# Transposing the tokens of six of eight experts on VectorE, from gathered quarter rows

## The chip, the cores and the metric

The kernel runs on one core of one Trainium2 chip. The core has TensorE (PE in the profile, with its weight loads as PEld), VectorE (DVE), ScalarE (ACT), GpSimd (POOL) and SyncE (SP), which run side by side and wait for each other by semaphores. The metric is the device time of one execution in microseconds (us).

## The reference

Attention over pooled keys and values makes 4608 rows x of 512 columns. A gate gives each row 8 logits; the pairs of row and expert are taken in falling order of their logits until each of the 8 experts has its 576 rows. Each expert then applies its two matrices to its rows.

```python
cap = N // E                      # 4608 // 8 = 576
for idx in np.argsort(-logits.flatten()):
    tok, e = (int(idx) // E, int(idx) % E)
    if assigned[tok] >= 0 or counts[e] >= cap:
        continue
    assigned[tok] = e
    counts[e] += 1
for e in range(E):
    mask = assigned == e
    h = np.maximum(x[mask] @ w1[e], 0.0)      # (576, 512) @ (512, 1024)
    out[mask] = h @ w2[e]                     # (576, 1024) @ (1024, 512)
```

## The kernel before

**Three parts.** The attention (class `Attention`) writes x to DRAM as `xd`. The routing (class `Routing`) finds one full expert after another, by a search that counts rows above thresholds: VectorE compares, TensorE counts, VectorE decides, several rounds per expert. It ends with the expert's number `eid` and with `rows`, the 576 row numbers as a tile of 128 partitions and 5 columns, tile t in column t (the fifth tile has 64 rows). The number of an expert below is its place in this order. The experts (class `Experts`) then multiply.

**One expert.** `gather` (L1031) fetches the 576 rows of `xd` into `xg` by five indirect DMAs that GpSimd issues, one token per partition, 2 KB each. TensorE contracts over partitions, so x has to be turned: `xt` (L1060) transposes tile t by four TensorE transposes of 128x128 into the PSUM tile `tp` (two buffers), chunk j of the result holding columns 128j to 128j+127. Every fp32 operand is split in two parts of TensorE's faster format: ScalarE copies `tp` to `xh` and VectorE writes the rest, `tp - xh`, to `xl`. The weights are split likewise, w1 into `w1h` and `w1l` and w2 into `w2h` and `w2l`, in eight pieces of 512 columns each (class `Pieces` in `experts`). `load_1` loads w1 so that partition p of chunk j holds row 128j + p, as x's columns lie.

`stage1` (L1075) computes the 1024 hidden columns in blocks f of 128, first for tokens 0 to 255, then for 256 to 575: 12 matmuls for each block (three products of high and low parts, four chunks j), into one of five PSUM banks `h`. After each block ScalarE writes `hh` and VectorE `hl`. `stage2` (L1113) multiplies tile by tile with w2, 24 matmuls each for four tiles, and a last half tile; ScalarE copies the result to `yt` (two buffers) and GpSimd scatters it by row number.

**The order.** Nothing reorders the program: each engine runs its instructions in the order in which the program issues them. The generators `stage1` and `stage2` yield after each matmul with an estimate of its time, and `experts` keeps a planned clock `now` and a planned end of VectorE's work `dve`. Between matmuls `advance` (L1263) puts in the next step of the routing of the following expert when its inputs are planned to be ready, `turns` (L1333) puts in the next tile's transpose, `Pieces.by` a piece of the weights, and `flush` those VectorE instructions that `later` has put off. `turns` asks that the rows are planned to have arrived (6.5 + 1.3t after the row numbers are known), that 1.4 us have passed since the last tile, and that a routing step has just been put in (`fresh`), that routing is over (`through`), or that the tile's limit `late` is reached. So tiles 0 to 2 of the next expert fall into the second stage of the present one, tiles 3 and 4 into its own first stage. The row numbers are taken into use only when the present expert's five tiles are turned, as there is one `xg`. No routing step starts while an `xl` is still put off (`first`, L1314).

The row numbers come out in `Routing.close` (L715): nine matmuls (L779) give sums in which every number stands at one place, `cp` holds them for the 18 groups of 32 places in two parts v, and eight matmuls with shifted copies of the matrix `spread` (L798) put four groups above each other in the partitions, which gives `rows`.

Of the kernel before, what the change touches and what calls it, by code (L numbers as in the profile page):

```python
# [9 lines left out]
F32 = mybir.dt.float32  # L10
# [413 lines left out]
class Routing:  # L424
# [56 lines left out]
    def more(self):  # L481
# [10 lines left out]
        nc.vector.tensor_scalar(self.spread[:, 96:128], t, 0.0, None, op0=OP.is_equal)  # L492

        self.blk = cst.tile([128, 20, NC], BF, name="blk")
        nc.scalar.activation(self.blk[:, :18], self.i36[:, 1:19, None].to_broadcast([128, 18, NC]), AF.Copy)
# [219 lines left out]
    def close(self, k, last):  # L715
# [58 lines left out]
        for b0, b1 in halves:  # L774
# [19 lines left out]
            t0, t1 = b0 // 4, b1 // 4  # L794
            ps = self.psum()
            for g in range(4):
                for v in range(2):
                    nc.tensor.matmul(ps[:, :t1 - t0], self.spread[:, 96 - 32 * g:224 - 32 * g], cpv[:, v, :, g],  # L798
                                     start=(g == v == 0), stop=(g == 3 and v == 1))
# [184 lines left out]
class Experts:  # L984
# [27 lines left out]

    def load_1(self, eid, q0=0, q1=4):
        nc = self.nc
        r = nc.sync.value_load(eid[0:1, 0:1], min_val=0, max_val=7)
        if q0 == 0:
            self.raw1.append(self.buf("raw1", [128, 4, 1024]))
        src = self.w1[ds(r, 1)].rearrange("o (j p) f -> p (o j) f", p=128)
        for q in range(q0, q1):
            nc.sync.dma_start(self.raw1[-1][:, *self.part(q)], src[:, *self.part(q)])  # L1020

    def load_2(self, eid):
# [4 lines left out]
        for i in range(0, 8, 2):  # L1027
            nc.sync.dma_start(raw[:, i:i + 2], src[:, i:i + 2])
        self.raw2.append(raw)

    def gather(self, rows, t0, t1):  # L1031
# [27 lines left out]

    def xt(self, t, name="tp", bufs=2, later=lambda after, t, f: f()):  # L1060

# [5 lines left out]
        ps = self.psA.tile([128, 4, 128], F32, name=name, bufs=bufs)  # L1067
        for j in range(4):
            nc.tensor.transpose(ps[:, j, :n], self.xg[:n, t, 128 * j:128 * j + 128], self.ident[:n, :n])  # L1069
        o = slice(128 * t, 128 * t + n)  # L1070
        nc.scalar.activation(self.xh[:, :, o], ps[:, :, :n], AF.Copy)  # L1071
        xl, xh = self.xl[:, :, o], self.xh[:, :, o].bitcast(F32)
        later(1.3, 0.65, lambda: nc.vector.tensor_tensor(xl, ps[:, :, :n], xh, op=OP.subtract))  # L1073

# [127 lines left out]
def experts(ctx, tc, g, R, xd, w1, w2, out, ident, cap, keep):  # L1202
# [15 lines left out]
    now, dve, ready = 0.0, 0.0, 0.0  # L1218

    def later(after, t, f):  # L1220

        waiting.append((now + after, t, f))
# [8 lines left out]
    def step(e):  # L1231

        nonlocal now, ready, dve, fresh, coming, through
        if held:
# [6 lines left out]
        if what == "id":  # L1241

            if p > e or p and pieces[p - 1].l < 8:
                held.append((p, crit, t, what))
                return False
            X.load_1(R.eid, 0, 4 if p else 2)
            eids[p] = R.eid
        elif what == "rows":
            if p and turned[p - 1] < 5:
                held.append((p, crit, t, what))  # L1250
                return False
            X.gather(R.rows, *R.found)
            if R.found[1] == 5:
# [9 lines left out]
    def advance(e, t, quiet=False):  # L1263

        nonlocal now, fresh
        now += t
        fresh = False
        while True:
            if waiting and waiting[0][0] <= now:
                flush(len(waiting) - 1)  # L1270
            elif ready > now or quiet or first(e) or not step(e):
                break
# [47 lines left out]
    def turn(e, t, name="tp", bufs=2):  # L1320

        nonlocal now
        now = max(now, since[e, "rows"] + 6.0 + 1.3 * t) + 0.45
        flush(1)
        X.xt(t, name, bufs, later_low)
        turned[e] = t + 1
# [6 lines left out]
    def turns(e, upto, late):  # L1333

        nonlocal last
        t = turned.get(e, 5)
        if t < upto and due(e, "rows", 6.5 + 1.3 * t) and now >= last + 1.4 and (fresh or through or t < late):
            last = now
            turn(e, t)
# [15 lines left out]
    for i in range(4):  # L1355
        w1.next(i < 3)
    since[0, "rows"] = -7.0

    step(0)
# [9 lines left out]
    for e in range(8):  # L1369
# [5 lines left out]
        for n, dt in enumerate(X.stage1(later, not e)):  # L1375
# [5 lines left out]
            if n == (84 if e else 40):  # L1381
                for t in range(turned[e], 5):
                    turn(e, t)
            if n >= 64 and n % 2:
                w2.by((n - 70) // 14 if n > 70 else 0)
# [117 lines left out]
```

## Time and profile before

| | |
|---|---|
| Median of 3 runs | 611.87 us (611.85 to 612.09) |
| The profiled execution | 612.35 us, its span 609.9 us |
| Mean granted clock of TensorE | 0.984 |
| HBM traffic | 72.53 MB read, 18.87 MB written |
| Attention and the first routing | about the first 157 us |
| One expert, window of the trace | 57.7 us early, 54.4 us late |

The profile names a group of instructions by line, engine, operation and tiles. Its chain of work is followed back from the last instruction to what released each step. A matmul's duration is its passage through a pipelined array, so the distance between starts shows what it takes from the next. In the timeline an instruction's row has its start, its duration, and in brackets how long its engine had been idle and what ended that.

### The profile page before, as it was taken

To read this page: it belongs to the slowest core of one execution; us is meant where nothing else is said; L and a number is where in the kernel's file an instruction comes from. 1 tells how busy PE (TensorE), PEld (TensorE's weight loads), DVE (VectorE), ACT (ScalarE), POOL (GpSimd) and SP (SyncE) were. 2 spreads that over 40 slices of the span, in tenths; PEclk is the share of its full clock that TensorE was granted. 3 is DMA by queue.
4 is the path that set the end of the run, shared out by engine and by line. 5 is a ranking of instruction groups with operands and counts; after the bars stand their busy time and mean duration, and the time that the engine had idled before them with its cause. 6 is when DMAs were issued, how large, how long until landed. Compare 5 with 4: busy or idle time off the path is not lost.

```text
span 609.9 us, 11520 instructions
## 1 busy us (share of the span) xinstructions
PE 591.5 (97%) x4340; PEld 518.3 (85%) x4340; DVE 396.1 (65%) x1164; ACT 240.0 (39%) x562; POOL 177.3 (29%) x222
## 2 busy tenths in 40 slices
PE   8999999985999999999999999999999999999996
PEld 5999999983797799779977987898799889888975
DVE  7578888987885778767964976487367328503500
ACT  7444444461461434233432452255135325513411
POOL 2999999001200500420312301130221123011012
PEclk9999999995999999999999999999999999999999
DMA  8999972223531740616403701540081037014011
GB/s 353 419 420 423 397 274 82 77 100 98 167 116 31 254 147 22 213 62 219 134 35 116 284 1 52 207 174 18 36 323 57 34 120 278 2 52 166 1 40 43
DMA packets 32641, 92.23 MB, mean 151 GB/s; under 512 B 3488, under 2 KB 3488, under 8 KB 29888
## 3 DMA queue, kind: packets, MB, share of 16 engines
q1 hardware_dynamic: 21296, 62.92, 27.5%
q0 software_dynamic: 5952, 19.01, 9.2%
q10 hardware_dynamic: 5328, 9.48, 4.1%
q8 instruction: 35, 0.57, 0.4%
q14 instruction: 30, 0.25, 0.1%
HBM read 72.53 MB, written 18.87 MB: 150 GB/s over the span
## 4 chain that ended last, share of the span: by engine, by line
PE 81%; issue 7%; DVE 4%; DMA 3%; POOL 3%; ACT 1%; SPq 0%; POOLq 0%; ACTq 0%; another core or an unknown queue 0%; DVEq 0%
PE h L1093 32%; PE h L1127 25%; PE psa L272 6%; PE pss L227 5%; PE h L1132 4%; PE tp L1069 3%; DMA rawk<-in_k_dram 2%; PE pse L256 2%; PE rt L256 1%; PE rt L668 1%; DMA out_dram<-yt,rows 1%; PE rt L630 1%; DMA xg<-xd,rows 1%; PE rt L217 1%; DVE e L238 1%
## 5 line engine op out<-in xcount | busy, mean ns | idle before, releaser
L1127 PE MATMUL h<-w2l,hh 128*128 128x512 f32 x256 | 101.8, 398 | 0.0
L1127 PE MATMUL h<-w2h,hh 128*128 128x512 f32 x256 | 101.4, 396 | 0.3 <-PEq L1193 0.3
L1127 PE MATMUL h<-w2h,hl 128*128 128x512 f32 x256 | 101.5, 396 | 0.0
L1107 POOL DMA_INDIRECT out_dram<-yt,rows x29 | 30.3, 1045 | 232.3 <-ACT yt L1141 231.9
L1098 ACT ACTIVATE hh<-h 128x320 fp32r<-128x320 f32 (+1 forms) x128 | 52.5, 410 | 106.6 <-PE h L1093 103.3
L1093 PE MATMUL h<-xh,w1h 128*128 128x320 f32 (+1 forms) x512 | 93.2, 301 | 0.2 <-ACT xh L1071 0.2
L1093 PE MATMUL h<-xl,w1h 128*128 128x320 f32 (+1 forms) x512 | 93.4, 300 | 0.0
L1101 DVE SCALAR_TENSOR_TENSOR hl<-h,hh 128x320 fp32r<-128x320 f32 (+1 forms) x128 | 57.2, 451 | 53.1 <-ACT hh L1098 34.6
L1093 PE MATMUL h<-xh,w1l 128*128 128x320 f32 (+1 forms) x512 | 91.0, 298 | 0.0
L1093 PEld LDWEIGHTS h<-xh,w1h 128*128 128x128 f32 x512 | 75.7, 190 | 3.4 <-issue 2.7
L1093 PEld LDWEIGHTS h<-xl,w1h 128*128 128x128 f32 x512 | 76.1, 190 | 0.4
L1093 PEld LDWEIGHTS h<-xh,w1l 128*128 128x128 f32 x512 | 75.8, 189 | 0.0
L1037 POOL DMA_INDIRECT xg<-xd,rows x40 | 39.3, 982 | 101.9 <-DVE halves L806 52.7
L1141 ACT ACTIVATE yt<-h 128x512 f32<-128x512 f32 x32 | 19.1, 598 | 112.1 <-PE h L1127 67.4
L272 PE MATMUL psa<-vblk,eT 128*128 128x146 f32 (+3 forms) x390 | 59.9, 302 | 0.2
L1127 PEld LDWEIGHTS h<-w2h,hh 128*128 128x128 f32 x256 | 48.2, 188 | 9.3 <-issue 0.7
L1127 PEld LDWEIGHTS h<-w2l,hh 128*128 128x128 f32 x256 | 48.3, 189 | 8.8
L1127 PEld LDWEIGHTS h<-w2h,hl 128*128 128x128 f32 x256 | 48.2, 188 | 8.8
L272 PEld LDWEIGHTS psa<-vblk,eT 128*128 128x128 f32 (+1 forms) x390 | 50.9, 180 | 1.8 <-issue 0.3
L1049 DVE TENSOR_TENSOR w1l<-raw,w1h 128x512 fp32r<-128x512 f32 x64 | 41.7, 685 | 13.4 <-ACT w1h L1045 13.1
L1073 DVE TENSOR_TENSOR xl<-tp,xh 128x512 fp32r<-128x512 f32 (+1 forms) x40 | 25.3, 633 | 37.4 <-ACT xh L1071 37.3
L1058 DVE TENSOR_TENSOR w2l<-raw,w2h 128x512 fp32r<-128x512 f32 x64 | 43.2, 682 | 2.0 <-ACT w2h L1055 1.8
(224 smaller groups left out, 903.3 us busy)
## 6 DMA issues: line engine op xcount, KB each, us to landing
raw<-in_moe_w_dram SPq DMA_DIRECT2D x64, 512.0 KB, 6.3
xd<-xt ACTq DMA_DIRECT2D x36, 256.0 KB, 5.6
rawv<-in_v_dram SPq DMA_DIRECT2D x7, 1280.0 KB, 14.1
rawk<-in_k_dram SPq DMA_DIRECT2D x7, 1152.0 KB, 11.7
rawq<-in_q_dram SPq DMA_DIRECT2D x7, 1152.0 KB, 11.8
rawk<-in_k_dram SPq DMA_DIRECT2D x2, 576.0 KB, 4.7
rawv<-in_v_dram SPq DMA_DIRECT2D x1, 768.0 KB, 8.0
rawq<-in_q_dram SPq DMA_DIRECT2D x1, 640.0 KB, 9.0
```

The source lines that it names most:

```text
L227: nc.tensor.matmul(ps[cols, j // 2, 144 * (j % 2):144 * (j % 2) + 144], self.q_of(b, j, n, cols.stop - cols.start), self.kblk[b % 4][:, j] ...
L272: self.nc.tensor.matmul(o[h], self.eT[i][:, c, h], self.vblk[b % 4][:, self.BLOCKS[c]:self.BLOCKS[c + 1]], start=(c == cs[0]), stop=(c == ...
L1037: nc.gpsimd.indirect_dma_start(out=self.xg[:n, t, :], out_offset=None, in_=self.xd, in_offset=bass.IndirectOffsetOnAxis(ap=rows[:n, t:t + ...
L1049: self.nc.vector.tensor_tensor(l, raw, h.bitcast(F32), op=OP.subtract)
L1058: self.nc.vector.tensor_tensor(self.w2l[:, i], self.raw2[e][:, i], self.w2h[:, i].bitcast(F32), op=OP.subtract)
L1073: later(1.3, 0.65, lambda: nc.vector.tensor_tensor(xl, ps[:, :, :n], xh, op=OP.subtract))
L1093: nc.tensor.matmul(ps[:, :m], a[:, j, fs], b[:, j, o], start=(n == 0), stop=(n == 11))
L1098: nc.scalar.activation(hh[:, f, o], ps[:, :m], AF.Relu)
L1101: later(0.65, 0.4, lambda f=f, o=o, m=m, ps=ps: nc.vector.scalar_tensor_tensor(hl[:, f, o], ps[:, :m], 0.0, hh[:, f, o].bitcast(F32), op0= ...
L1107: st = nc.gpsimd.indirect_dma_start(out=rows, out_offset=bass.IndirectOffsetOnAxis(ap=idx, axis=0), in_=y, in_offset=None)
L1127: nc.tensor.matmul(ps, a[:, f, o], b[:, f], start=(f == 0 and k == 0), stop=(f == 7 and k == 2))
L1132: nc.tensor.matmul(ps[64 * a:64 * a + 64, :256], self.hr[:, f], self.raw2[e][:, f, 256 * a:256 * a + 256], start=(f == 0), stop=(f == 7))
```

## The change

For the experts from the third on (`quarters(e)`: e > 1), each row of `xd` is fetched as four quarter rows of 128 columns. Group n of 32 places is fetched by one indirect DMA of 128 pieces: partition 32a + i receives quarter a of the row at place 32n + i, so 18 indirect DMAs bring the 576 rows. The numbers of the quarters, `quarters` (128 partitions, 18 columns), come from two more matmuls and one more VectorE instruction in `close`, with two constants, `copies` and `acol`, made in `more`.

In this layout one VectorE instruction turns a tile: within each group of 32 partitions it transposes 32x32 blocks of `xg`, taking every fourth column, straight into `tp`. Chunk j of the result holds in partition p the column 4p + j. To match, `load_1` loads w1 for these experts so that partition p of chunk j holds row 4p + j. Experts 0 and 1, and the slow path `experts_one_by_one`, keep the old way.

The planner no longer issues the fetches at once: `fetch` puts one out per 1.3 us of planned time between the matmuls, starting 1.5 us after the row numbers, and `landed` holds when a tile is planned to be there, 3.7 us after its last fetch. A tile of these experts is turned when that has passed by 0.5 us and VectorE is planned to be free, or when its limit is reached; it adds 0.7 us to VectorE's planned time and none to TensorE's. Its `xl` is put off by 1.5 us instead of 1.3. All `xl` put off are now written out by matmul 7 and by matmul 103 of the first stage (7 and 55 for expert 0).

```diff
+        self.copies = cst.tile([128, 4, 32], F16, name="copies")
+        nc.vector.tensor_scalar(self.copies, self.spread[:, None, 96:128].to_broadcast([128, 4, 32]), 4.0, None, op0=OP.mult)
+        t = cst.tile([128, 1], I32, name="ta")
+        nc.vector.tensor_scalar(t, self.pq, 5, None, op0=OP.arith_shift_right)
+        self.acol = cst.tile([128, 1], F32, name="acol")
+        nc.vector.tensor_scalar(self.acol, t, -4.0, None, op0=OP.add)
...
             ps = self.psum()
+            if k > 1:
+                for v in range(2):
+                    nc.tensor.matmul(ps[:, 16:34], self.copies.rearrange("p a i -> p (a i)"), cp[:, v, :18],
+                                     start=(v == 0), stop=(v == 1))
+                self.quarters = wk.tile([128, 18], I32, name="quarters", bufs=3)
+                nc.vector.tensor_scalar(self.quarters, ps[:, 16:34], self.acol, 0.0, op0=OP.add, op1=OP.max)
             for g in range(4):
...
-        src = self.w1[ds(r, 1)].rearrange("o (j p) f -> p (o j) f", p=128)
+        src = self.w1[ds(r, 1)].rearrange("o (p j) f -> p (o j) f" if quarters else "o (j p) f -> p (o j) f", p=128)
...
+    def quarter(self, idx, n):
+        if not n:
+            self.xg = self.buf("xg", [128, 5, 512])
+        t, g = divmod(n, 4)
+        self.nc.gpsimd.indirect_dma_start(out=self.xg[:, t, 128 * g:128 * g + 128], out_offset=None,
+                                          in_=self.xd.rearrange("n (a d) -> (n a) d", a=4),
+                                          in_offset=bass.IndirectOffsetOnAxis(ap=idx[:, n:n + 1], axis=0))
...
         ps = self.psA.tile([128, 4, 128], F32, name=name, bufs=bufs)
-        for j in range(4):
+        if quarters:
+            nc.vector.transpose(ps[:, :, :n].rearrange("p j (g i) -> p g j i", i=32),
+                                self.xg[:, t, :4 * n].rearrange("p (g i j) -> p g j i", j=4, i=32))
+        for j in range(0 if quarters else 4):
             nc.tensor.transpose(ps[:, j, :n], self.xg[:n, t, 128 * j:128 * j + 128], self.ident[:n, :n])
...
-        later(1.3, 0.65, lambda: nc.vector.tensor_tensor(xl, ps[:, :, :n], xh, op=OP.subtract))
+        later(1.5 if quarters else 1.3, 0.65, lambda: nc.vector.tensor_tensor(xl, ps[:, :, :n], xh, op=OP.subtract))
...
+    def fetch():
+        nonlocal pace
+        e, n, idx = wanted.pop(0)
+        X.quarter(idx, n)
+        pace = max(pace, now) + 1.3
+        if n % 4 == 3 or n == 17:
+            landed[e, n // 4] = pace + 3.7
...
-            X.gather(R.rows, *R.found)
+            if quarters(p):
+                wanted.extend((p, n, R.quarters) for n in range(18))
+                pace = max(pace, now + 1.5)
+            else:
+                X.gather(R.rows, *R.found)
+                for t in range(*R.found):
+                    landed[p, t] = now + 6.0 + 1.3 * t
...
         now += t
         fresh = False
+        if wanted and now >= pace:
+            fetch()
...
-        nonlocal now
-        now = max(now, since[e, "rows"] + 6.0 + 1.3 * t) + 0.45
+        nonlocal now, dve
+        while (e, t) not in landed:
+            fetch()
+        now = max(now, landed[e, t])
         flush(1)
-        X.xt(t, name, bufs, later_low)
+        if quarters(e):
+            dve = max(dve, now) + 0.7
+        else:
+            now += 0.45
+        X.xt(t, name, bufs, later_low, quarters(e))
...
-        if t < upto and due(e, "rows", 6.5 + 1.3 * t) and now >= last + 1.4 and (fresh or through or t < late):
+        if t < upto and now >= landed.get((e, t), now + 1) + 0.5 and now >= last + 1.4 and (
+                t < late or (dve <= now if quarters(e) else fresh or through)):
...
+            if n in ((7, 103) if e else (7, 55)) and lows:
+                flush()
```

More of the change, by code (lines that the diff above doesn't have):

```diff
@@ L1011, in piece, with load_1 @@
         return slice(i % 4, i % 4 + 1), slice(512 * (i // 4), 512 * (i // 4) + 512)
-    def load_1(self, eid, q0=0, q1=4):
+    def load_1(self, eid, q0=0, q1=4, quarters=False):
         nc = self.nc
@@ L1058, in low2, with xt @@
         self.nc.vector.tensor_tensor(self.w2l[:, i], self.raw2[e][:, i], self.w2h[:, i].bitcast(F32), op=OP.subtract)
-    def xt(self, t, name="tp", bufs=2, later=lambda after, t, f: f()):
+    def xt(self, t, name="tp", bufs=2, later=lambda after, t, f: f(), quarters=False):
         nc = self.nc
@@ L1218, in experts, with quarters @@
     now, dve, ready = 0.0, 0.0, 0.0
+    wanted, landed, pace = [], {}, 0.0
+    def quarters(e):
+        return e > 1
+    def fetch():
[5 more added lines that the diff above has]
+            landed[e, n // 4] = pace + 3.7
     def later(after, t, f):
@@ L1231, in step @@
     def step(e):
-        nonlocal now, ready, dve, fresh, coming, through
+        nonlocal now, ready, dve, fresh, coming, through, pace
         if held:
@@ L1245, in step @@
                 return False
-            X.load_1(R.eid, 0, 4 if p else 2)
+            X.load_1(R.eid, 0, 4 if p else 2, quarters(p))
             eids[p] = R.eid
@@ L1357, in experts @@
     since[0, "rows"] = -7.0
+    landed.update({(0, t): 1.3 * t - 1.0 for t in range(5)})
     step(0)
```

## The prediction

> **What bounds the kernel now.** I read the page first (busy times, then the chain of work that ended last). All times are microseconds of one profiled execution.
>
> ```profile
> span 609.9 us, 11520 instructions
> ...
> PE 591.5 (97%) x4340; PEld 518.3 (85%) x4340; DVE 396.1 (65%) x1164; ACT 240.0 (39%) x562; POOL 177.3 (29%) x222
> ```
> ```profile
> PE 81%; issue 7%; DVE 4%; DMA 3%; POOL 3%; ACT 1%; SPq 0%; POOLq 0%; ACTq 0%; another core or an unknown queue 0%; DVEq 0%
> ```
>
> TensorE (PE) is busy 97% of the span and holds 81% of the chain. Next I read one line, that of the transposes which the change takes from PE, and then PE's timeline around them, because matmuls overlap: the 273 ns of one is its passage through the array, not the time that it takes from its neighbours.
>
> ```profile
> L1069 PE MATMUL tp<-ident,xg x160: 220/273/356, 153.8 to 554.2; 128*128 128x128 f32 x128, 64*128 64x64 f32 x32
> ```
> ```profile
> 420.27 0.39 PE L1127 MATMUL h<-w2l,hh 128*128 128x512 f32 x1
> 420.50 0.18 PE L680 MATMUL rt<-cnt,fold 128*128 128x8 f16 x1
> 420.54 0.64 PE L1069 MATMUL tp<-ident,xg 128*128 128x128 f32 x4
> 420.93 0.48 PE L1127 MATMUL h<-w2h,hh 128*128 128x512 f32 x1
> 421.25 0.40 PE L1127 MATMUL h<-w2h,hl 128*128 128x512 f32 x1
> ```
> ```profile
> 426.89 0.40 PE L1127 MATMUL h<-w2l,hh 128*128 128x512 f32 x1
> 427.12 0.18 PE L680 MATMUL rt<-cnt,fold 128*128 128x8 f16 x1
> 427.16 0.47 PE L1127 MATMUL h<-w2h,hh 128*128 128x512 f32 x1
> 427.48 0.39 PE L1127 MATMUL h<-w2h,hl 128*128 128x512 f32 x1
> ```
>
> Starts are what counts. The second group shows a routing matmul alone between expert matmuls: two expert matmuls need 427.48 - 426.89 = 0.59 where two starts lie 0.23 apart without it, so it costs about 0.13, nearly all of it the slower restart. In the first group four transposes of one tile follow such a matmul: 421.25 - 420.27 = 0.98. The tile itself therefore costs PE 0.98 - 0.59 = 0.39; the restart is paid by the routing matmul, which stays.
>
> **Part 1: what goes from PE.** Experts 2 to 7 have five tiles each, 30 in all. In the PE timeline 22 stand directly behind a routing matmul (first and last of them here), eight stand alone (485.47 the first, 553.93 the last): the first three of expert 6 and all of expert 7, where routing is over.
>
> ```profile
> 259.49 0.64 PE L1069 MATMUL tp<-ident,xg 128*128 128x128 f32 x4
> ...
> 503.96 0.46 PE L1069 MATMUL tp<-ident,xg 64*128 64x64 f32 x4
> ```
> ```profile
> 485.24 0.39 PE L1127 MATMUL h<-w2h,hl 128*128 128x512 f32 x1
> 485.47 0.60 PE L1069 MATMUL tp<-ident,xg 128*128 128x128 f32 x4
> 485.82 0.48 PE L1127 MATMUL h<-w2l,hh 128*128 128x512 f32 x1
> 486.14 0.39 PE L1127 MATMUL h<-w2h,hh 128*128 128x512 f32 x1
> ```
> ```profile
> 553.93 0.46 PE L1069 MATMUL tp<-ident,xg 64*128 64x64 f32 x4
> ```
>
> Alone, with its own restart, a tile costs (486.14 - 485.24) - 2 x 0.23 = 0.44. So 22 x 0.39 = 8.6 and 8 x 0.44 = 3.5: **12.1 leave PE**. PE is the path there, since the rows around run start to start without a gap.
>
> **Part 2: what comes to PE.** Two matmuls of 18 columns per expert, beside the eight of the row numbers.
>
> ```profile
> 396.04 0.36 PE L798 MATMUL rt<-cp,spread 128*128 128x5 f16 x8
> ```
>
> Eight pass in 0.36, at most 0.045 each; 12 x 0.03 = **0.4 added**, without a new restart since they ride with these eight. VectorE then reads the same PSUM tile for the quarter numbers. Whether the eight wait for that read isn't visible before; I take 0, since the columns differ, and as the upper end six waits of one read, about 0.3 each: 1.8.
>
> **Part 3: VectorE.** Each tile brings one block transpose of 128x512 from SBUF to PSUM. No row shows one. The nearest is the subtraction that reads the same PSUM tile at the same size, 0.69. The lower end is 0.23, an instruction that turns out a quarter of the columns; the upper end is 16 blocks in each group of 32 partitions, each paid like the smallest instruction, 0.15: 2.4. I take 0.69, by the nearest row.
>
> ```profile
> 8.32 0.23 DVE L484 TENSOR_SCALAR tri<-jp 128x128 bf16<-128x128 int32 x1
> ```
> ```profile
> 420.73 0.15 DVE L687 TENSOR_TENSOR g<-rt,need 32x8 bf16<-32x8 f32 x1 [1.89 <-PE rt L680]
> ```
> ```profile
> L1073 DVE TENSOR_TENSOR xl<-tp,xh 128x512 fp32r<-128x512 f32 x32 | 22.0, 687 | 35.9 <-ACT xh L1071 35.8
> ```
> ```profile
> 214.80:272.50 57.70, 57.70 (x429) 49.63 (x427) 43.83 (x139) 21.25 (x50) 10.97 (x15) 1.00 0.34 114
> 272.50:330.20 57.70, 57.70 (x427) 49.30 (x427) 41.33 (x137) 21.24 (x50) 10.34 (x15) 1.00 0.34 115
> ```
>
> The windows are one expert each; the columns are PE, PE loads, VectorE, ScalarE, GpSimd. VectorE is busy 43.8 of 57.7 in the stretch where expert 2's first tiles fall, 41.3 in the next. Four full transposes and a half one add 4.5 x 0.69 = 3.1. That fits in the 13.9 that are free, so by itself it costs nothing; at 2.4 it would be 10.8 of the 13.9, and the cover would be nearly gone.
>
> The Trainium skill, "VectorE: DVE Perf Modes", The three transpose paths, gives 390 ns on TensorE and 311 ns on VectorE for 128x128 in bf16, and its Rules for kernel authors prefer TensorE for a full 128x128 block whose target is PSUM (VectorE only within 32x32). As an estimate from that page, four blocks would be 1.24 a tile on VectorE; the sum stays the same, with 5.6 of the free 13.9 used. The rule would have this work stay where it is; the rows above show the engine that it would stay on to be the full one.
>
> **Part 4: the gathers.** Five gathers per expert become 18, each of 128 pieces of 512 B, and they wait on nothing new but sit in GpSimd's queue among the scatters of the results.
>
> ```profile
> L1037 POOL DMA_INDIRECT xg<-xd,rows x40: 914/960/1392, 150.3 to 513.2; - x40
> ```
> ```profile
> 250.02 0.98 POOL L1037 DMA_INDIRECT xg<-xd,rows  x1 [33.15 <-DVE rows L802]
> ...
> 256.30 1.01 POOL L1107 DMA_INDIRECT out_dram<-yt,rows  x1 [0.22 <-ACT yt L1141]
> ```
> ```profile
> 293.11 0.98 POOL L1037 DMA_INDIRECT xg<-xd,rows  x1 [18.93 <-DVE halves L806]
> ```
> ```profile
> xg<-xd,rows POOLq DMA_INDIRECT x40, 3.8
> ```
>
> A gather takes 0.96 at the median and 0.91 at least, though every fifth has half the rows, so the price is per instruction. Five and what lies between fill 250.02 to 256.30: 1.26 each, 18 take 22.7. A scatter takes 1.0, with its gaps about 1.4. Expert 3's gathers can start at 293.1, and its first stage at 330.2 by the window above: 37 for 22.7 + 4 x 1.4 + 3.8 = 32. Covered. **Expert 2 is the tight one.** Its first gather can start at 250.0 and the first stage of expert 2 starts at 272.4.
>
> ```profile
> 272.43 0.38 PE L1093 MATMUL h<-xh,w1h 128*128 128x256 f32 x1
> ...
> 286.18 0.75 PE L1093 MATMUL h<-xh,w1h 128*128 128x320 f32 x4
> ```
>
> Expert 1's five scatters now stand between the gathers: the last gather ends near 250.0 + 22.7 + 5 x 1.4 = 279.7 and has landed some 3 later (3.8 from its issue): 282.7. The first two tiles, eight gathers and two scatters, land near 266: in time. Tiles 3 and 4 are used from 286.18, which moves forward by the five tiles removed, to 284.1. The last tile needs 282.7 + 0.7 for the transpose, and as much again for the copy to xh: 284.1. So PE is just about reached. Worse, the planner paces gathers at 1.3 and counts nothing for scatters, so the transposes of tiles 3 and 4 are put into VectorE's queue 2 to 4 too early and wait there at its head. Behind them stand hl of the first stage, the next expert's counts and comparisons of the routing, and the xl of the tile; ScalarE waits with xh. PE's five h banks let it run on without hl for a few groups; a routing matmul placed in that stretch isn't covered. I take 1.0, bounds 0 and 4. Once only, by expert 3's margin.
>
> The Trainium skill, "GPSIMD Engine Reference", Specifications, says that the SBUF interface is shared with VectorE and contended by VectorE instructions with two SBUF inputs. By that, gathers beside w1l and w2l would be longer; the row shows 914 to 1392 ns for all 40, so the trace knows this at most as 0.4 on single ones. The rival below prices it from rows.
>
> **Part 5: loads and start.** w1 in rows 4p+j keeps pieces of 2 KB (512 columns) and the same count, only the order of rows differs.
>
> ```profile
> raw<-in_moe_w_dram SPq DMA_DIRECT2D x64, 512.0 KB, 6.3
> ```
>
> The planner uses them no sooner than 9 after it has their number (`due(e, "id", 9)`), against 6.3: cost 0; at double the time the first pieces would be 3.6 late, once per expert at most. At the start VectorE gets three small instructions beside tri (L484 above).
>
> ```profile
> 13.68 1.22 POOL L195 TENSOR_TENSOR vblk<-vsum,mask 128x128 f32<-128x128 f32 x3 [10.95 <-DVE vsum L187]
> 15.35 2.62 POOL L172 TENSOR_TENSOR tk<-rawk 128x1152 f32<-128x1152 f32 x1 [0.45 <-DMA rawk<-in_k_dram]
> ```
>
> Three like tri are at most 0.7, about 0.55 since two are smaller; GpSimd waits for VectorE at 13.68 and then has 0.45 to spare before the DMA that heads the chain: **0.1 added**.
>
> **The sum.** 612.35 (span 609.9 and 2.45 around it) - 12.1 + 0.4 + 0.1 + 1.0 = 601.75. The median of the three runs is 611.87, 0.48 lower: 601.3.
>
> **The rivals.**
> Full cover: the head-of-queue wait at expert 2 falls where PE has no routing matmul. Then 1.0 goes, and some restarts behind single tiles too: 599.3 to 600.3. For it: five banks and idle VectorE. Against it: routing of expert 3 runs in that stretch.
>
> VectorE becomes late in several experts: the transpose costs nearer 2.4, or the eight matmuls wait for the quarter read behind a queue of hl. With one instruction of 0.69 ahead of that read, six waits of 0.3 + 0.69 give 6; at 2.4 a tile, 1.7 more than taken, experts 2 and 3 are late by that on up to two tiles each: 7. 603 to 608. For it: VectorE feeds every routing matmul. Against it: 13.9 free even in the busiest expert.
>
> GpSimd too slow, slower than before: if a gather of 512-byte pieces takes g from start to start instead of 1.26, expert 2 loses 1.0 + 18 x (g - 1.26). The 11.6 that are left without that term are gone at g = 1.86; at 2.1 the time is 600.3 + 1.0 + 15 = 616. The longest gather in the trace, 1.39 and 0.3 to the next, would give 609. For it: the issue is software on one engine, and transfers beside w1's load differ. Against it: 40 gathers and 40 scatters all near 1.
>
> That the transposes stay on PE is excluded by the code: for experts 2 to 7 the loop over them is empty. No change would need the wait at expert 2 to be just as long as the gain.
>
> **Chances.** My case (600.3 to 602.7) 0.5; full cover 0.22; VectorE late 0.2; about even 0.03; GpSimd too slow 0.05. The range of 599.0 to 607.0 leaves out the lower edge of full cover, the top of VectorE late, and the last two. A difference under 0.2% (1.2 us) can't be told from no change: faster 0.92, same 0.03, slower 0.05.
>
> **What would show it.** PE's timeline without L1069 after expert 1, and each expert window about 2 shorter; transposes at 0.6 to 0.75; PE's waits still near zero but for one near 278 to 285. Wrong would be: PE rows that wait for VectorE in every expert, gathers above 1.4, or ScalarE's xh waiting for a transpose that waits for its gather in experts 3 to 7.

## The result, and the profile after

The change makes the kernel slower: 678.47 us median of 4 runs (675.00 to 680.29) against 611.88, a ratio of 1.108 (95% interval 1.103 to 1.113). The forecast was 601.3. The profiled execution of the changed kernel took 676.87. In its line numbers L1049 is the quarter gather, L1091 the block transpose, L1096 and L1098 are xh and xl, L1118 is the first stage, L1152 and L1157 are the second, L675 to L703 the routing search, L805, L808 and L811 the quarter numbers (matmul, VectorE's read) and the row numbers behind them.

First the page of the changed kernel (span, busy times), its chain of work, and the rows of the cores view that give the mean granted clock, of after and then of before:

```profile
span 675.1 us, 11440 instructions
...
PE 606.8 (90%) x4232; PEld 526.9 (78%) x4232; DVE 427.3 (63%) x1203; ACT 237.9 (35%) x562; POOL 253.2 (38%) x300
```
```profile
PE 57%; DVE 13%; issue 11%; DMA 9%; POOL 4%; another core or an unknown queue 3%; ACT 3%; POOLq 0%; ACTq 0%; DVEq 0%
```
```profile
core 0: 675.1 us, clock 0.940
```
```profile
core 0: 609.9 us, clock 0.984
```

TensorE has the 108 instructions fewer that were forecast (4340 to 4232), but it is now idle for 675.1 - 606.8 = 68.3 where it was idle for 18.4: 49.9 more. And its clock fell. 0.060 of 675.1 against 0.016 of 609.9 are 40.5 and 9.8 lost to the gate, 30.7 more. 49.9 + 30.7 less the 12.1 of the transposes are 68.5, and the span grew by 65.2. The 30.7 is an estimate and a little high, since it counts the clock inside the gaps too: the busy time, without the 12.1, grew by 606.8 - 591.5 + 12.1 = 27.4. So the question is what makes TensorE idle; the clock falls behind some of these gaps (a row below).

Next the stages, in the windows view (columns: window, its length, PE, PE loads, VectorE, ScalarE, GpSimd busy, granted clock, DMA share, GB/s). Each window runs from one expert's last half tile to the next one's. Before:

```profile
268.80:326.60 57.80, 57.80 (x429) 49.38 (x428) 42.25 (x140) 21.76 (x51) 10.59 (x15) 1.00 0.34 115
...
494.00:548.60 54.60, 54.53 (x361) 48.34 (x360) 24.78 (x58) 21.02 (x50) 10.49 (x15) 1.00 0.34 121
548.60:601.70 53.10, 52.80 (x332) 46.63 (x331) 13.46 (x30) 15.39 (x39) 5.29 (x10) 1.00 0.18 64
```

and after:

```profile
267.50:344.60 77.10, 63.08 (x402) 54.03 (x401) 49.93 (x143) 22.94 (x54) 28.59 (x34) 0.89 0.27 90
...
547.80:614.30 66.50, 56.62 (x343) 49.28 (x342) 30.75 (x65) 20.83 (x50) 22.84 (x28) 0.92 0.29 99
614.30:666.30 52.00, 51.70 (x322) 45.79 (x321) 13.94 (x31) 15.20 (x39) 5.31 (x10) 1.00 0.19 66
```

Expert 2 takes 19.3 longer and expert 6 still 11.9, though VectorE is busy only 30.75 of 66.50 there. Expert 7, in whose stage nobody gathers, is 1.1 shorter. About 2 was forecast for a whole expert, but before only two tiles were turned in this window, by the prediction's prices 0.9. The two new groups of instructions, in the lines view by form (busy, mean ns, idle before):

```profile
L1091 DVE STREAM_TRANSPOSE tp<-xg 128x512 f32<-128x512 f32 x24 | 26.4, 1098 | 0.2 <-issue 0.2
```
```profile
L1049 POOL DMA_INDIRECT xg<-xd,quarters x108 | 105.0, 972 | 122.2 <-DVE quarters L808 90.8 <-issue 30.8 <-DMA xg<-xd,quarters 0.6
```

A gather costs GpSimd about what was forecast, 0.97 and 0.30 to the next. A transpose takes 1.10, not 0.69. Neither explains the timeline of TensorE while expert 7's gathers run (start, length; idle time before it in brackets):

```profile
577.69 0.31 PE L1118 MATMUL h<-xl,w1h 128*128 128x320 f32 x1 [1.10 <-issue]
...
581.88 0.69 PE L1118 MATMUL h<-xh,w1l 128*128 128x320 f32 x2 [0.97 <-issue]
583.98 0.69 PE L1118 MATMUL h<-xh,w1l 128*128 128x320 f32 x2 [1.41 <-issue]
...
586.83 0.42 PE L1118 MATMUL h<-xl,w1h 128*128 128x320 f32 x1 [1.89 <-issue]
```

These are matmuls of one accumulation, their operands long there; "issue" says that nothing which the profile shows holds them. And at the first quarter gathers of all, before any block transpose, TensorE's timeline and VectorE's stand so:

```profile
265.97 0.39 PE L675 MATMUL rt<-oh,cmp 128*128 128x32 bf16 x9
266.21 0.47 PE L1152 MATMUL h<-w2h,hl 128*128 128x512 f32 x1
...
270.75 1.51 PE L1157 MATMUL h<-raw,hr 128*64 128x256 f32 x11 [0.62 <-issue]
```
```profile
263.74 0.75 DVE L632 TENSOR_TENSOR cmp<-q16a,j 128x1152 bf16<-128x1152 f16 x1
270.81 0.19 DVE L679 TENSOR_TENSOR diagc<-rt,dq 128x32 f32<-128x32 f32 x1 [6.32 <-remote]
```

L679 needs only L675, which ended at 265.97 + 0.39 = 266.36. VectorE went on 4.45 later, and in that time TensorE worked. So not only do matmuls start late; the news that one has ended comes late too.

### The profile page after: what moved, and what is told of

The parts are those of the page before. It is cut to its first block, busy times and chain, and to the rows that moved or that the text cites. A ratio compares the mean times of both kernels' runs of the same rounds, so it can differ in the third digit from the quotient of the medians.

```text
span 675.1 us, 11440 instructions
## 1 busy us (share of the span) xinstructions
PE 606.8 (90%) x4232; PEld 526.9 (78%) x4232; DVE 427.3 (63%) x1203; ACT 237.9 (35%) x562; POOL 253.2 (38%) x300
## 4 chain that ended last, share of the span: by engine, by line
PE 57%; DVE 13%; issue 11%; DMA 9%; POOL 4%; another core or an unknown queue 3%; ACT 3%; POOLq 0%; ACTq 0%; DVEq 0%
PE h L1118 22%; PE h L1152 14%; DMA out_dram<-yt,rows 7%; PE psa L272 6%; PE pss L227 5%; POOL xg L1049 3%; PE h L1157 3%; PE pse L256 2%; DVE tp L1091 1%; POOL out_dram L1132 1%; PE rt L256 1%; DVE hl L1126 1%; DVE w1l L1071 1%; ACT xh L1096 1%
## 5 line engine op out<-in xcount | busy, mean ns | idle before, releaser
L1049 POOL DMA_INDIRECT xg<-xd,quarters x108 | 105.0, 972 | 122.2 <-DVE quarters L808 90.8
L1118 PE MATMUL h<-xh,w1h 128*128 128x320 f32 (+1 forms) x512 | 100.9, 314 | 11.6 <-issue 6.3
L1132 POOL DMA_INDIRECT out_dram<-yt,rows x29 | 30.7, 1058 | 199.3 <-ACT yt L1166 197.3
L1118 PE MATMUL h<-xl,w1h 128*128 128x320 f32 (+1 forms) x512 | 100.0, 315 | 6.0 <-issue 6.0
L1152 PE MATMUL h<-w2h,hh 128*128 128x512 f32 x256 | 102.9, 402 | 0.3 <-PEq L1218 0.3
L1152 PE MATMUL h<-w2h,hl 128*128 128x512 f32 x256 | 102.8, 402 | 0.0
L1152 PE MATMUL h<-w2l,hh 128*128 128x512 f32 x256 | 101.9, 398 | 0.0
L1118 PE MATMUL h<-xh,w1l 128*128 128x320 f32 (+1 forms) x512 | 97.1, 311 | 4.4 <-issue 4.4
L1118 PEld LDWEIGHTS h<-xh,w1h 128*128 128x128 f32 x512 | 81.4, 202 | 16.2 <-issue 9.7
L1118 PEld LDWEIGHTS h<-xl,w1h 128*128 128x128 f32 x512 | 82.2, 204 | 11.0 <-issue 10.9
L1118 PEld LDWEIGHTS h<-xh,w1l 128*128 128x128 f32 x512 | 81.0, 202 | 8.0 <-issue 8.0
L1152 PEld LDWEIGHTS h<-w2h,hh 128*128 128x128 f32 x256 | 49.0, 191 | 9.9 <-issue 0.7
L1152 PEld LDWEIGHTS h<-w2l,hh 128*128 128x128 f32 x256 | 49.2, 192 | 9.5
L1152 PEld LDWEIGHTS h<-w2h,hl 128*128 128x128 f32 x256 | 49.1, 192 | 9.3 <-issue 0.5
L1166 ACT ACTIVATE yt<-h 128x512 f32<-128x512 f32 x32 | 19.1, 597 | 96.0 <-PE h L1152 68.5
L1096 ACT ACTIVATE xh<-tp 128x512 fp32r<-128x512 f32 (+1 forms) x40 | 22.2, 556 | 83.4 <-DVE tp L1091 64.7
```

Of the source, the lines that this page charges most:

```text
L1049: self.nc.gpsimd.indirect_dma_start(out=self.xg[:, t, 128 * g:128 * g + 128], out_offset=None, in_=self.xd.rearrange("n (a d) -> (n a) d", ...
L1118: nc.tensor.matmul(ps[:, :m], a[:, j, fs], b[:, j, o], start=(n == 0), stop=(n == 11))
L1132: st = nc.gpsimd.indirect_dma_start(out=rows, out_offset=bass.IndirectOffsetOnAxis(ap=idx, axis=0), in_=y, in_offset=None)
L1152: nc.tensor.matmul(ps, a[:, f, o], b[:, f], start=(f == 0 and k == 0), stop=(f == 7 and k == 2))
```

## The experiments

All runs were timed against the kernel before on the same chip (611.7 to 611.9). The cuts show only the lines that matter. Theory G: the gathers do the harm. Rival V: VectorE's transposes and the waits on them. Rival Q: TensorE's wait for VectorE's read of the quarter numbers.

**First set: one part undone at a time.**

Five gathers of 128 whole rows, issued at once, in place of the quarters; everything else of the change kept:
```diff
-                wanted.extend((p, n, R.quarters) for n in range(18))
+                X.gather(R.rows, 0, 5, True)
```


> The kernel after, with one part undone: from the third expert on x comes by five gathers of whole rows (2 KB pieces) at once instead of 18 paced gathers of quarter rows. VectorE's block transposes, the quarter numbers and w1 in rows 4p+j stay. x is then not laid out in quarters, so the output is not the reference's. Theory G (the 18 gathers of 512-byte pieces do the harm: while they run, semaphore updates arrive late and all engines wait): 600 to 608 us, no L1126 or L1123 wait longer than 3 us, expert stages back at 53 to 57 us. Rival V (VectorE's transposes at 1.10 us and the copies to xh that wait for them do it): 660 to 678 us, as the kernel after. Rival Q (TensorE's wait for VectorE's read of the quarter numbers): also unchanged, since that read stays.

Measured: 615.7 us. 62.8 of the change's time go with the quarter gathers, so G carries most. But 615.7 lies above the range that G gave, so something of V or Q is left.

TensorE's transposes put back, the 18 gathers kept:
```diff
-        for j in range(0 if quarters else 4):
+        for j in range(4):
```


> The kernel after, with the other part undone: 18 quarter gathers stay, but TensorE transposes the tiles (four 128x128 each) as before, and VectorE's block transposes are gone. The quarters are then in the wrong order, so the output is not the reference's. Theory G: still slow, 675 to 700 us (the kernel after plus 0 to 12 us of transposes back on TensorE), with delayed updates in the same stretches. Rival V: 612 to 620 us.

Measured: 698.2 us, as G expected, and 19.7 more than after. V doesn't carry the main loss.

18 gathers of 32 whole rows (the last two of 64):
```diff
-        ...(out=self.xg[:, t, 128 * g:128 * g + 128], ... ap=idx[:, n:n + 1]
+        ...(out=self.xg[32 * g:32 * g + 32, t, :], ... ap=idx[:32, t:t + 1]
```


> The kernel after, with its 18 gathers per expert at the same places and pace, but each of 32 whole rows (32 pieces of 2 KB; 64 rows for the last two) instead of 128 pieces of 512 bytes; the same 32 row numbers serve every gather of a tile, so the output is not the reference's. Everything else stays. If the number of pieces does the harm (G, pieces): 600 to 612 us. If the number of gather instructions does it (G, instructions): 665 to 680 us. Rival V: 665 to 680 us.

Measured: 691.0 us, above both ranges. A quarter of the pieces, and no better: this speaks for the number of gather instructions. Why it is 12.5 slower than after isn't shown.

The quarter numbers last:
```diff
-            if k > 1:  (two matmuls, VectorE's read)
             for g in range(4):  (eight matmuls of the row numbers, then that of the counts)
+            if k > 1:  (two matmuls, VectorE's read)
```


> The kernel after, with the two matmuls of the quarter numbers and VectorE's read of them put behind the eight matmuls of the row numbers and that of the counts, so that none of these waits for the read; the output is the reference's. Rival Q: the 6 waits of L811 (7.0 us of TensorE and 7.7 us of its loads in the trace after) and what follows them go: below 650 us. Theory G and rival V: 665 to 680 us, at most the 7 us of the waits themselves less.

Measured: 661.0 us, 17.4 less than after, a miss for both sides. The waits view of after has

```profile
PE rt L811 <- DVE quarters L808: 7.0, 6, 2.3
```

and one of the six, in the timelines of TensorE and VectorE and in the windows view, is

```profile
497.64 0.35 PE L811 MATMUL rt<-cp,spread 128*128 128x5 f16 x8 [2.28 <-DVE quarters L808]
```
```profile
497.37 0.23 DVE L808 TENSOR_SCALAR quarters<-rt,acol 128x18 int32<-128x18 f32 x1
```
```profile
498.30:501.80 3.50, 3.50 (x19) 3.50 (x18) 1.74 (x9) 1.53 (x4) 2.67 (x3) 0.51 0.20 57
```

VectorE reads the numbers only when the transpose, three hl and an xl ahead of them in its queue are done; TensorE stands 2.28, and the granted clock is then about one half for 3.5, which costs another 1.7. The Trainium skill, "TensorE: Matmul & The Clock Gate", Part 1, puts the half clock behind an idle window of about 3.4 us. Here 2.28 were enough. They aren't always: behind the same wait for the next expert the clock stays full.

```profile
563.94 0.35 PE L811 MATMUL rt<-cp,spread 128*128 128x5 f16 x8 [2.28 <-DVE quarters L808]
```
```profile
564.00:567.50 3.50, 3.50 (x35) 3.50 (x35) 1.66 (x7) 2.32 (x5) 2.73 (x3) 1.00 0.34 112
```

So Q is real, but the 17.4 aren't all its own. The gain lies in experts 5 and 6, whose windows (56.8 and 56.3) are 9.5 and 10.2 shorter than in after, while that of expert 3 is 5.8 longer; a wait with its half clock is 4.0. The rest is that the same gathers cost less there. In this run 16 of them start between 559.39 and 579.29, as close as in after, and TensorE is full until 579.2 (windows view of the run):

```profile
559.40:579.20 19.80, 19.78 (x122) 18.62 (x121) 9.57 (x24) 7.63 (x22) 15.31 (x15) 1.00 0.20 56
```

In after the same stretch of 16 begins at 564.16, with the first gap 10.9 behind its start. Why the order of a few small matmuls changes that isn't shown.

**Second set: gathers alone.** These are the kernel before, unchanged but for further transfers into a buffer that nobody reads.
```diff
+        if wanted and now >= pace:
+            n, idx = wanted.pop(0)
+            X.spare(idx, n)
+            pace = max(pace, now) + 1.3
```


> The kernel before, and nothing of the change, but from the third expert on 18 further gathers of 128 quarter rows into a small buffer that nobody reads, one each 1.3 us, begun 8 us after the five gathers of the rows. Nothing waits for them. Backlog theory (gathers issued back to back for more than about 9 us hold up TensorE and its semaphore updates, whoever reads them): slower by 25 to 60 us, with gaps of TensorE from about 9 us after the start of each burst until 2 to 3 us after its end. Rival (the gathers cost only because the transposes wait for them): within 3 us of the kernel before.

Measured: 698.2 us, 86.3 slower, more than expected. No engine's work waits for these gathers, no transpose has moved, and it is worse than the whole change (which has 78 gathers more than before, this run 108). GpSimd's timeline (the first of the five of the rows and the last of 18 gathers in a row), the windows view and TensorE's timeline of one burst:

```profile
514.15 0.98 POOL L1045 DMA_INDIRECT xg<-xd,rows  x1 [8.45 <-DVE halves L806]
...
535.54 0.95 POOL L1035 DMA_INDIRECT xq<-xd,rows  x1 [0.30 <-issue]
```
```profile
500.30:514.20 13.90, 13.90 (x131) 12.20 (x131) 6.95 (x21) 3.78 (x9) 2.08 (x4) 1.00 0.70 244
514.20:523.50 9.30, 9.30 (x71) 9.30 (x70) 6.61 (x27) 2.79 (x7) 7.17 (x8) 1.00 0.77 268
523.50:539.50 16.00, 4.93 (x14) 3.06 (x14) 3.16 (x14) 1.58 (x6) 10.03 (x12) 0.66 0.18 48
```
```profile
533.98 0.43 PE L1101 MATMUL h<-xh,w1h 128*128 128x320 f32 x1 [1.69 <-issue]
535.37 0.43 PE L1101 MATMUL h<-xh,w1l 128*128 128x320 f32 x1 [0.96 <-issue]
536.78 0.62 PE L1101 MATMUL h<-xh,w1l 128*128 128x320 f32 x1 [0.99 <-issue]
```

For the first 9.3 of the burst TensorE is full. From then until 3.0 after the last gather's end it passes 14 matmuls in 16.0, with the DMA share at 0.18: the DMA engines aren't full. The matmuls then start about 1.4 apart here, and about 0.70, 1.4 or 2.1 apart over the whole stretch (in the timeline of after, too), so TensorE gets on in steps of 0.70.

The same at half the rate (`+ 2.6`):

> The same 18 further gathers per expert in the kernel before, but one each 2.6 us instead of 1.3. Backlog theory: the harm is a matter of rate, so within 5 us of the kernel before and no gaps of TensorE over 0.5 us in the expert stage. Rival (a fixed price for each gather, 66 us over 78 further ones, 0.85 each): as slow as with 1.3 us, 60 us or more above the kernel before.

Measured: 654.7 us, between the two. Rate matters, but the harm isn't gone: in the trace the spare gathers run into those of the rows and the scatters of the results, in bursts of 11 and 12.

Plain transfers of as many bytes from the same queue, planned at 1.3, and gathers of 16 rows:
```diff
-        self.nc.gpsimd.indirect_dma_start(out=self.xq[:, n % 4, :], ...
+        self.nc.gpsimd.dma_start(self.xq[:, n % 4, :], self.xd[128 * (n % 9):128 * (n % 9) + 128, :128])
```
```diff
-        ...(out=self.xq[:, n % 4, :], ... ap=idx[:, n % 5:n % 5 + 1]
+        ...(out=self.xq[:16, n % 4, :], ... ap=idx[:16, n % 5:n % 5 + 1]
```


> The kernel before with 18 further transfers per expert from GpSimd's queue at 1.3 us, as in the run of 698.2 us, but plain ones of the same 128 pieces of 512 bytes without row numbers from SBUF. If what holds up TensorE is that a transfer is issued by GpSimd at all (its descriptors, its semaphore updates): slower by 30 us or more. If it is the indirect form: within 5 us of the kernel before.

> The run of 698.2 us with gathers of 16 quarter rows (8 KB) each instead of 128. If the harm is a price of each gather whatever its size, as the runs with 128 pieces of 512 bytes and 32 pieces of 2 KB suggest (698.2 and 691.0 us): 680 us or more. If it goes with the number of rows: below 630 us.

Measured: 611.9 us (ratio 1.0005, 0.9995 to 1.0014) and 701.6 us. The lines view of the first and of the second, and from the first a row of GpSimd's timeline and the windows view:

```profile
L1035 POOL DMA_DIRECT2D xq<-xd x108 | 58.5, 552 | 16.5 <-DMA xq<-xd 12.6 <-issue 3.4
```
```profile
L1035 POOL DMA_INDIRECT xq<-xd,rows x108 | 95.6, 885 | 35.3 <-issue 31.7 <-DMA xq<-xd,rows 3.6
```
```profile
459.39 2.23 POOL L1035 DMA_DIRECT2D xq<-xd x4
```
```profile
493.90:548.50 54.60, 54.53 (x363) 48.33 (x362) 24.79 (x58) 20.97 (x50) 20.54 (x33) 1.00 0.41 143
```

108 plain transfers cost nothing, though they follow each other even faster than the gathers, 0.56 apart where four come in a row; 108 gathers with an eighth of the rows cost as much as full ones. It is the form with row numbers, per instruction.

Two bursts of six, meant to stand alone:
```diff
+            pace = max(pace, now) + (1.3 if n != 5 else 10.0)
```


> The kernel before with 12 further gathers per expert that nobody reads, 72 in all, at 1.3 us as in the run of 698.2 us, but in two bursts of six with 10 us between them, the first 14 us after the gathers of the rows. If it is the length of a burst that decides (gaps of TensorE began 8 to 10 us after the start of one): within 5 us of the kernel before. If each further gather has a price (0.80 at a spacing of 1.3 us, 0.40 at 2.6): 640 to 670 us.

Measured: 642.7 us, in the range of a price for each gather. But the condition wasn't met: from expert 4 on the first six of each followed the five of the rows without a pause. So once more, six per expert and later (`pace = now + 24.0`):

> The kernel before with six further gathers per expert that nobody reads, 36 in all, at 1.3 us, begun late enough to lie apart from the five gathers of the rows: in the run of 642.7 us the first six of each expert had run into these, and gaps of TensorE stood in those joined bursts of 11 (8.9 to 9.4 us after their start) and not in the bursts of six. If the length of a burst decides: within 4 us of the kernel before. If each further gather has a price of 0.40 or more: 626 us or more.

Measured: 620.8 us, neither. Most of the loss lies in experts 2 to 4 (windows 61.2, 60.4 and 59.1 long, before 57.8, 56.5 and 56.6), where stretches of seven and eight still formed; the windows of experts 5 and 6 are those of before, though stretches of six and seven stand there too:

```profile
450.70:505.10 54.40, 54.40 (x361) 48.40 (x360) 29.58 (x83) 20.83 (x50) 15.96 (x21) 1.00 0.37 129
505.10:559.70 54.60, 54.53 (x361) 48.33 (x360) 24.73 (x58) 20.94 (x50) 16.60 (x21) 1.00 0.37 128
```

Counted over the traces of before and of the five runs with spare gathers, from 160 us on (a burst: starts of gathers and scatters at most 1.75 apart; a gap: over 0.25 of TensorE from 1 after its first start to 4 after its last):
```
length of burst   bursts   with a gap   mean sum of gaps, us
1 to 3            164       0            0.0
4 to 6             32       8            0.3
7 to 9             33      13            0.7
10 to 12           14      14            3.9
17 and 18           7       7           10.9
```
In the bursts of 18 the first gap comes 9.0 to 9.6 after the start. So in these six traces the price grows with length, as if something filled while gathers follow each other at 1.25. There is no sharp border, and between 4 and 9 it isn't settled what decides. Nor does length alone decide above that: the 16 of the run of 661.0 stand against it.

**Third set: VectorE alone.** The first run (615.7) without the quarter numbers, so that only transposes, loads and the planner are left of the change; then the same from the sixth expert on (`return e > 4`):

> The run with five gathers of whole rows (615.7 us), and the quarter numbers left out too: their two matmuls per expert and VectorE's read of them. VectorE's transposes and w1 in rows 4p+j are then all that is left of the change; the output is not the reference's. If the read of the quarter numbers is what kept that run from the 601.3 of the prediction: 600 to 606 us. If VectorE's transposes (1.10 us against 0.69 taken) and ScalarE's wait for them are: 610 to 616 us.

> The run of 614.4 us (VectorE's transposes with gathers of whole rows, no quarter numbers), but only from the sixth expert on, where the routing search has ended or nearly so; the output is not the reference's. If those 614.4 come from a VectorE that is late beside the search in the third to fifth experts: 605 to 609 us. If the transposes cost the same wherever they stand: 611 to 613 us.

Measured: 614.4 us (ten runs, 611.1 to 615.9) and 606.5 us (ratio 0.991, 0.990 to 0.993), both as the theory of a late VectorE has it. The first in the windows view, and one of its gaps in the timelines of TensorE and VectorE:

```profile
378.00:438.00 60.00, 57.95 (x385) 49.74 (x384) 42.30 (x121) 20.49 (x50) 10.11 (x15) 0.94 0.32 112
438.00:496.80 58.80, 56.63 (x387) 48.59 (x386) 42.10 (x121) 20.59 (x50) 10.29 (x15) 0.97 0.34 111
496.80:552.70 55.90, 54.04 (x341) 47.94 (x340) 41.97 (x105) 22.93 (x55) 10.12 (x15) 0.97 0.37 125
```
```profile
449.72 0.39 PE L675 MATMUL rt<-oh,cmp 128*128 128x32 bf16 x9 [1.62 <-DVE cmp L632]
...
451.26 0.39 PE L1112 MATMUL h<-xh,w1l 128*128 128x256 f32 x1 [0.55 <-DVE w1l L1065]
```
```profile
448.92 0.75 DVE L632 TENSOR_TENSOR cmp<-q16a,j 128x1152 bf16<-128x1152 f16 x1
```

VectorE is back to back there: transposes and xl of the first tiles, w1l, hl and the search's comparison stand in one queue, and TensorE waits for the comparison. Idle 2.1, 2.2 and 1.9, and a clock 0.06, 0.03 and 0.03 below full over these lengths, are 6.1 + 7.0 = 13.1, an estimate: about as much as lies between 614.4 and the forecast. Later there is room (the second run, windows and lines view):

```profile
493.30:545.40 52.10, 52.10 (x343) 46.54 (x342) 30.60 (x64) 20.82 (x50) 10.26 (x15) 1.00 0.38 130
```
```profile
L1085 DVE STREAM_TRANSPOSE tp<-xg 128x512 f32<-128x512 f32 x12 | 13.1, 1093 | 0.0
```

52.1 where before has 54.6: 2.5 less, where about 2 was forecast, with transposes at 1.09 and TensorE without a gap. The Trainium skill, "VectorE: DVE Perf Modes", Rules for kernel authors, would leave a full block bound for PSUM to TensorE. By these two runs it is right beside the routing search and wrong behind it.

**Fourth set: other forms of the whole change.** Numbers last, gathers spaced by 2.3:
```diff
-        pace = max(pace, now) + 1.3
+        pace = max(pace, now) + 2.3
```


> The changed kernel with the quarter numbers read last (as in the run of 661.0 us) and one constant more: the planner spaces the quarter gathers by 2.3 us instead of 1.3. The output is the reference's. Backlog theory: the gaps of TensorE without a cause go, 605 to 630 us, the rest of the loss being tiles that now come late (18 gathers take 41 us). Fixed price for each gather: 655 us or more.

Measured: 633.2 us, between its two ranges. The windows view, and the waits view of 270 to 290:

```profile
268.60:346.10 77.50, 60.66 (x410) 51.30 (x409) 49.31 (x145) 21.61 (x51) 28.28 (x35) 0.89 0.27 90
...
467.10:519.20 52.10, 52.10 (x343) 46.56 (x342) 37.66 (x94) 20.96 (x51) 24.25 (x29) 1.00 0.37 128
```
```profile
DVE tp L1091 <- DMA xg<-xd,quarters: 8.8, 1, 8.8
```

The late experts have the whole gain. In expert 2 eighteen gathers at 2.3 need 41 us; it now waits for its rows instead. So the change was left to later experts, from the fifth, fourth, sixth and seventh on (`return e > 3`, 2, 4, 5):

> The kernel of the run of 633.2 us (quarter numbers read last, gathers spaced by 2.3 us), but quarter rows only from the fifth expert on; the third and fourth take x by whole rows and TensorE's transposes as before. The output is the reference's. In the run of 633.2 us the stages from the fifth expert's on took 52.1, 52.1 and 52.0 where the kernel before has 54.4, 54.6 and 53.1, and all the loss stood in the third and fourth. If that holds without them: 604 to 608 us, faster than the kernel before. If the gain there came only from work that the slow stages had pulled forward: 611 to 616 us.

> The same from the fourth expert on. The third expert's lateness (18 gathers in the 19 us between its row numbers and its stage) is gone, the fourth has 37 us for 18 gathers of 2.3, 41 us. If the loss of the run of 633.2 us was that of the third expert and what it left behind: 603 to 610 us. If the fourth expert's last tiles are late too: 612 to 620 us.

> The kernel of the run of 617.2 us (quarter numbers read last, gathers spaced by 2.3 us) with quarter rows only from the sixth expert on; the output is the reference's. In that run the stages behind the fifth expert's took 53.4, 52.1 and 52.0 where the kernel before has 54.4, 54.6 and 53.1. If the loss there belonged to the routing search that VectorE still runs beside the fifth expert's tiles: 606 to 609 us, faster than the kernel before. If the first expert with quarters always loses: 612 to 618 us.

> The same from the seventh expert on: two experts of eight keep the change, both at times when VectorE has the most room (26.9 us busy of 67 in the window 481 to 548 of the kernel before). Routing search as the cause: 607 to 610 us. First expert always loses: 612 to 618 us.

Measured: 617.2, 631.7, 612.2 (ratio 1.0007, 0.9998 to 1.0016) and 610.6 us (0.9982, 0.9973 to 0.9991). The first two are above all that was expected: the window of the first expert with quarters is 64.5 and 73.2 long, where before has 56.6 and 56.5, and the gain of the later ones doesn't make up for it. The third lies where a first expert with quarters was expected to lose in any case, the fourth between its two ranges. The farther the quarters keep from the routing search, and the fewer experts have them, the less is lost; only the last form beats the kernel before, by 1.1 us. A wider spacing of 2.9, from the sixth expert on:

> The kernel of the run of 612.2 us (quarter rows from the sixth expert on, numbers read last) with the gathers spaced by 2.9 us instead of 2.3; the output is the reference's. Without the quarter gathers the same transposes gave 606.5 us. If what stands between is still gathers that follow each other too fast: 607 to 610 us. If 18 gathers now end too late (52 us, nearly the whole stage of an expert): 612 to 620 us.

Measured: 634.4 us, a miss: 18 gathers of 2.9 no longer fit, and the waits view of 570 to 590 shows TensorE waiting for xh of a tile whose rows are late:

```profile
PE h L1118 <- ACT xh L1096: 8.9, 1, 8.9
```

## Why the prediction was wrong

**Part 1** held: 108 instructions fewer, and 1.7 and 2.5 (52.6 and 52.1 against 54.3 and 54.6) in the two whole stages where nothing else stands in the way.

**Part 4 is the step that failed.** It read the price of a gather off GpSimd's own row ("the price is per instruction ... 18 take 22.7 ... Covered") and checked only who waits for the rows. The rate came true. What was missing is a price to others: the rival of a gather slower than 1.86 (1.85 by its own formula) looked at the wrong engine. Spare gathers alone cost 86.3, whole rows in their place win 62.8 back, against the 1.0 that was taken. The trace of before has at most seven in a row and couldn't show this; that 18 in a row lay outside everything it contained was to be seen, and belonged in the range.

"Covered" was also reckoned with start times of before, and the change moves them. Expert 2's quarter gathers start at 257.75, not 250.0, and the last of them at 288.54, where it was to have ended at 279.7. Expert 3's begin 26 before its stage, not 37, and the last one starts 6.7 behind it. Row by row (GpSimd's timeline of after, TensorE's, and GpSimd's in the run of 612.2, where expert 3 keeps whole rows and still begins 16 later than before):

```profile
321.90 0.94 POOL L1049 DMA_INDIRECT xg<-xd,quarters  x1 [32.41 <-DVE quarters L808]
...
354.90 0.96 POOL L1049 DMA_INDIRECT xg<-xd,quarters  x1 [0.30 <-issue]
```
```profile
348.19 0.51 PE L1118 MATMUL h<-xh,w1h 128*128 128x256 f32 x2
```
```profile
309.08 0.98 POOL L1059 DMA_INDIRECT xg<-xd,rows  x1 [34.27 <-DVE rows L815]
```

So part of the 62.8 is plain lateness of rows: expert 2's window is 77.1 in after, 55.4 with whole rows, and still 77.5 with gathers spaced by 2.3. How much of the 62.8 is lateness and how much the hold-up wasn't separated, nor which condition of the planner moves the row numbers.

**Part 2** took 0 for the eight matmuls behind the read, with 1.8 and 6 as ends. They did wait, six times, 7.0 in all, more than either end; the order of the numbers is worth 17.4 in this kernel, not all of it through the waits. The term was priced by the read itself and one instruction, not by the whole of what stands ahead of it in VectorE's queue.

**Part 3** took 0.69 and cost 0, because 3.1 fit into 13.9 free. The transpose takes 1.10, inside its bounds, but the free time isn't where the tiles fall: 13 lost with no quarter gather involved. The rival of a late VectorE named this mechanism, and 603 to 608 was too little for it, since it priced no half clock; it also put the loss in experts 2 and 3, where the run of 614.4 has it in 4 to 6.

**Part 5** held as far as seen: with w1 in rows 4p+j three stages ran at 52.0 to 52.6.

By steps, from the forecast: 601.3 + 13.1 (VectorE, to 614.4) + 1.3 (quarter numbers, to 615.7; within the spread of these two runs) + 62.8 (18 gathers, to 678.5). Of the last, 17.4 hang on the order of the numbers; the terms aren't independent.

## What to carry to other kernels

Before one transfer is split into many, look how many of that kind already follow each other without a pause in the trace; beyond that number the engine's own row need not give the price, and a spare copy of the transfers that nobody reads measures it in one run. Times read off the trace of before hold only for what the change leaves in its place. Free time of an engine is worth what is free in the stretch where the new work falls, and what stands ahead in its queue is part of every wait for it. An idle gap of two microseconds on TensorE can bring 3.5 us of half clock behind it (2.28 did once and once didn't), so the range should hold both.

## What the runs showed of the hardware

Gathers by row numbers from GpSimd, 1.25 us from start to start, hold up TensorE when many follow each other: in the kernel before, with spare gathers, all 21 stretches of ten or more had gaps; in one of the longest 14 matmuls passed in 16.0 us. In one form of the change 16 in a row left TensorE full for 19.8 us, so something else has a part in it. Neither fewer rows (16 instead of 128: 701.6 us) nor larger pieces (691.0 us) eased it, and the end of a matmul reached VectorE 4.45 us late. Plain transfers from the same queue, as many and of the same size, did nothing of the kind (611.9 us), and took 0.55 instead of 0.98 of GpSimd. What fills up inside the chip stays open: no view names it, and the gaps are told as "issue" and "remote". All times here, the medians too, are of runs whose span and clock were recorded; whether the recording has a part in the hold-up isn't shown.
